# A two-layer spectral and MLP kernel: four plain groups instead of six, statistics scratch in PSUM, and a new order of the second pair's products

## The chip, the cores and the metric

One Trainium2 chip, one of its NeuronCores. The metric is the device time of one execution in microseconds (us). Engines are called PE (TensorE), DVE (VectorE), ACT (ScalarE), POOL (GpSimd) and SP (the queue that issues most DMAs).

## What is computed

The input x has 2048 tokens of 1024 features, in bf16. Four blocks follow one another, each added to its input: a spectral filter A, an MLP B, A again, and B again with the same weights.

```python
def _A_ref(x, w_r, w_i):
    X = rfft2(x, axes=(-2, -1))          # over tokens and features
    return irfft2(X * (w_r + 1j * w_i), s=(S, D)).astype(bf16)

def _B_ref(x, w1, b1, w2):               # D = 1024, F = 3584
    h = einsum("bsd,df->bsf", x, w1) + b1
    act = h * tanh(log1p(exp(-abs(h))) + where(h > 0, h, 0))   # Mish
    return einsum("bsf,fd->bsd", act, w2)

x = x + _A_ref(_layernorm(x), w_r, w_i)
x = x + _B_ref(_layernorm(x), w1, b1, w2)
x = x + _A_ref(_layernorm(x), w_r, w_i)
x = x + _B_ref(_layernorm(x), w1, b1, w2)
```

## The kernel before, in words

**Order and waits.** The program is written out by hand in one order; every engine gets its instructions in that order and runs them one after the other. A small class (Res) records who wrote and who read each buffer, and each instruction gets the semaphore waits that follow. DMAs queue in the same way on the engine that issues them: one that waits holds back all behind it on that queue.

**Tiles.** x stays in on-chip memory as 16 tiles of 128 tokens (XS). Layer B works on chunks of four tiles (512 tokens): pair 1 is chunks 0 and 1 (tiles 0 to 7), pair 2 chunks 2 and 3. A tile is normalised by statistics (stats_dve on DVE or stats_act on ACT, sums_to_mv, scales or root) and apply, and is then transposed into XT, by PE (transposed, L1109) or by DMA (normal, turned and turn).

**Hidden stage.** F is cut into 14 groups of 256. In pair 1, groups 0 to 5 are plain: mm1 (L1148) multiplies one chunk, 16 matmuls of 512 columns or twice as many of 256, and ACT applies Mish (L1152). These use banks 0 to 2 in rotation. Groups 6 to 13 of pair 1, and all 14 of pair 2, use Strassen's scheme in Winograd's form (quads): seven products of four 512-column matmuls (L1186), on sums of weight blocks (S1 to S4) and of token blocks (T1 to T4), in place of eight. A11, A12, A21 and A22 are the weight blocks, B11 and B21 the two halves of the first chunk, B22 a half of the second. DVE combines the products (add, L1191), ACT copies the first product out of its bank (L574) and applies Mish (L1196). token_sums (L1163) forms T1 to T4 on DVE from both chunks; T3 overwrites a part of the second chunk, so it waits until the plain products have read it.

**Weight sums.** In the first layer POOL makes S1 to S4 for each group with four additions (L1081 in fill_slot) and stores the slot to w1s_scratch; the second layer only loads it. For pair 1 the first four slots (early) lie where the tile of the inverse transform (UT) was, the next three (ws) where the plain weights were. POOL's first addition waits for a "gate", the normalisation of tiles 6 and 7 on DVE.

**Output stage.** products multiplies the hidden values by w2, again with seven Strassen products as stages of 4 tiles x 14 matmuls (L1268). STD and BACK are orders of these stages, BACK for pair 2 of the first layer. A stage's last product completes a half of a tile: in BACK B21 (stage 6) completes chunk 2 and T4 (stage 7) chunk 3. extra then takes statistics, normalises the tile, writes it to xn_scratch from POOL (xn_store) and reads it back from SP in the order that the next transform wants (xr_load, into XR); the last tile is copied there directly by 16 small DMAs (xr_direct). Meanwhile spin keeps PE busy with filler matmuls (L652). The next layer's first transform (s1, L635) reads XR in two halves and is drained by ACT (L641) and DVE (L643).

Of the kernel before, what the change touches and what calls it, by code (L numbers as in the profile page):

```python
# [7 lines left out]
P = 128  # L8
# [172 lines left out]
class KB:  # L181
# [274 lines left out]
    def sums_to_mv(self, j0, n):  # L456

        rs = self.r_mv[j0:j0 + n]
        mv, sq = self.MV[:, j0:j0 + n, :], self.RS[:, 1, j0:j0 + n]
        rr = self.r_rs[j0:j0 + n]  # L460

        def on(fn):
            self.op(self.dve, fn, reads=rs, writes=rs + rr)
        on(lambda e: e.tensor_scalar(mv, self.BN[:, j0:j0 + n, 0:2], 1.0 / self.D, None, op0=ALU.mult))
        on(lambda e: e.tensor_tensor(sq, mv[:, :, 0], mv[:, :, 0], ALU.mult))
        on(lambda e: e.tensor_tensor(mv[:, :, 1], mv[:, :, 1], sq, ALU.subtract))
# [27 lines left out]
    def scales(self, j0, n):  # L494

        rr = self.r_rs[j0:j0 + n]
        h, a, r = (self.RS[:, i, j0:j0 + n] for i in range(3))
        var = self.MV[:, j0:j0 + n, 1]
# [42 lines left out]
    def xr_load(self, j):  # L541
        self.dma(self.sp, self.XR.ap[row_of(j, 0):row_of(j, 7) + 1:4, :, :], self.xn_d[j], f"xl{j % 4}",
                 reads=[self.r_xnd[j]], parts=self.r_xr[1:3])

    def xr_direct(self, j, b, parts, queues):

        i = 0
# [147 lines left out]
    def layer_A(self, li):  # L695
# [189 lines left out]
        def open_ut():  # L885
            self.UT = self.alloc("UT", o["UT"], [P, P])

            self.r_ut = self.sub_res(self.UT, "ut", 4, o["UT"], P * P * 2)
# [61 lines left out]
        self.w1_buf = [self.alloc(f"W1_{i}", (self.ob["WS"] + i * 4096, 140 * K)[i > 4], [8, 256]) for i in range(6)]  # L950
        for fg in range(6):
# [119 lines left out]
    def fill_slot(self, b, fg, after=()):  # L1071
# [5 lines left out]
        self.load_w1(b.raw, fg, [b.res])  # L1077
        A = lambda n: self.wblock(b, n)
# [6 lines left out]
    def layer_B(self, li, last):  # L1085
# [91 lines left out]

        def quads(fgs, slot_of, B, after, lead=None):

            sums = open_sums()  # L1180

            def product(n, bank, a, b, start):
# [5 lines left out]
                            for db in range(4)], reads=[s.res, s.rs] + list(res), writes=[self.r_bank[bank]])  # L1188
# [9 lines left out]

            def parts(n):
                a, b, d = (3 * (n % 2) + i for i in range(3))  # L1200
                return a, b, d, sums[n % 2], sums[2 + n % 2], sums[4], 2 * fgs[n]

            N = len(fgs)
            for n in range(N + 1):
                if n < N:
                    a, b, d, p1, u2, u3, ft = parts(n)
                    product(n, a, "A11", "B11", True)
                    self.copy(act, p1.ap, PS[:, a, :], [self.r_bank[a]], [p1.res])
                    product(n, b, "S2", "T2", True)
                    add(u2, b, p1)  # L1210
                if n == N and lead:
                    lead()
                if n:
                    _, pb, pd, q1, q2, q3, pft = parts(n - 1)
                    mish(1, pft + 1, q3.ap, q3.res)
                    product(n - 1, pb, "A22", "T4", False)
                    add(q1, pb, q1)
                    mish(0, pft + 1, q1.ap, q1.res)
                    product(n - 1, pd, "S4", "B22", False)
                    add(q2, pd, q2)  # L1220
                    mish(1, pft, q2.ap, q2.res)
                    after(n - 1)
                if n < N:
                    product(n, d, "S1", "T1", True)
                    product(n, a, "A12", "B21", False)
                    mish(0, ft, PS[:, a, :], self.r_bank[a])
                    product(n, b, "S3", "T3", False)
                    add(u3, b, p1)
                    add(u3, d, u3)
# [7 lines left out]
        def load_w2(name, k, slot, prog=sp):  # L1237
# [5 lines left out]
            else:  # L1243
# [7 lines left out]
        BACK = (("A11", "B11", 0, True), ("S", "T3", 1, True), ("A21", "T1", 0, True), ("A11", "T2", 1, True), ("S", "B22", 0, False),  # L1251
                ("A12", "B21", 0, True), ("A22", "T4", 1, False))
# [181 lines left out]
        for j in range(4, 8):  # L1434
            residual(j)
# [5 lines left out]
        for fg in range(1, 4):  # L1441
            mm1(0, fg, 1)
            if fg > 1:
                self.stats_act(4 + fg)
        mm1(0, 4)
        at_tiles(1)
        mm1(0, 5, mid=turns(1, 0, 1))
# [6 lines left out]
        early = self.open_slots("WE", self.ob["W2"], 0, 1, 2, 3)  # L1454
        for n in range(4):
            self.fill_slot(early[n], 6 + n, [gate])
        for fg in range(2):
            mm1(1, fg, 0, mid=turns(1, 2, 3) if fg else ())
        for fg in range(2):
# [7 lines left out]
        for fg in range(2, 6):  # L1467
            if fg in (2, 4, 5):
                ws += self.open_slots("WS", self.ob["WS"], len(ws))
                self.fill_slot(ws[-1], 9 + len(ws))  # L1470
            mm1(1, fg)
            if fg == 2:
                token_sums(0, last=False)
            if fg == 3:
                for j in range(8, 12):
                    residual(j)
        order = early + ws + early[:1]
        B = token_sums(0)
        self.xn_buf = self.xn_out + [self.alloc(f"XN{i}", self.ob["XN2"] + i * 2048, [self.D]) for i in range(2)]

        def after(n):
            if n == 0:
                self.fill_slot(order[7], 13)
            if 1 <= n < 4:
                load_b(STD, n // 3, (n - 1) % 2)
            if n < 4:
                self.stats_dve(8 + n)
            if n == 4:
                self.scales(8, 4)
            if n > 3:  # L1490
                normal(4 + n)
                turn(4)
            for j in ((), (), (), (), (), (12, 13), (14,), (15,))[n]:
                residual(j)
        quads(list(range(6, 14)), order, B, after, lead)
        self.junk = self.alloc("JUNK2", self.ob["JUNK2"], [self.D])
        self.xn_buf = [self.alloc(f"XN{i}", self.ob["XN12"] + i * 2048, [self.D]) for i in range(2)] + self.xn_out
        w2 = {}
# [150 lines left out]
```

## Time and profile before

| quantity | value |
|---|---|
| median of 3 runs | 938.51 us (937.23 to 938.64) |
| the profiled execution | 936.66 us |
| its span, first to last instruction | 934.9 us |
| granted PE clock | 0.987 of full |
| first layer B, from the first plain product to the last output product | 122 to 476 us |
| pair 1's Strassen hidden stage, first layer | 172 to 223 us |
| from the last product to the second layer A's first transform | 476 to 488 us |
| second layer B, from the first plain product | 579 to 933 us |

The timeline gives start and duration of runs of like instructions; "x24" is their number, and the bracket says how long the engine had been idle before and what ended that. In the chain of work, each piece is what released the next one. "mean ns" of a matmul is longer than its step, because matmuls are pipelined; the step comes from a run of them divided by their number. SPq is the DMA-issuing part of SP.

### The profile page before, as it was taken

Reading aid. Unit: us, or ns where it says so; the run is one execution under the profiler, and the core shown is the slowest. Engines: PE = TensorE matmul, PEld = TensorE weight load, DVE = VectorE, ACT = ScalarE, POOL = GpSimd, SP = SyncE. Lnnn points to the kernel's source line nnn. Section 1 sums busy time; section 2 is a strip of 40 time slices with the busy share of each in tenths; the row PEclk is TensorE's granted clock in tenths of the full one; section 3 lists DMA queues with packets and bytes.
Section 4 is the critical chain, followed back from the end, with each engine's and each line's share of the span. In section 5 each row is a group of like instructions: output and inputs, shape, how many; then the busy total and the mean of one; then the engine's idle time right before and its main releaser. Section 6 shows DMA issues by size and latency. Waiting matters only on the chain.

```text
span 934.9 us, 13481 instructions
## 1 busy us (share of the span) xinstructions
PE 875.9 (94%) x5473; PEld 471.7 (50%) x5473; DVE 619.1 (66%) x973; ACT 427.5 (46%) x623; POOL 159.0 (17%) x183
## 2 busy tenths in 40 slices
PE   0799799999999999999979987999999999999998
PEld 0577486444444444444437765754444444444443
DVE  7698468686889667568746865647746665554473
ACT  7798485456203485510008975745551015552000
POOL 4922004950005642000130200000000000000000
PEclk9999999999999999999999997999999999999999
DMA  9969854676895488274640797433255635832432
GB/s 288 265 227 300 204 151 131 216 249 171 268 274 196 164 314 296 91 261 142 241 133 32 227 228 196 158 118 119 54 190 175 207 113 193 279 118 78 171 127 110
DMA packets 146335, 174.68 MB, mean 187 GB/s; under 512 B 66248, under 2 KB 125736, under 8 KB 146152
## 3 DMA queue, kind: packets, MB, share of 16 engines
q1 hardware_dynamic: 133424, 127.48, 44.5%
q0 software_dynamic: 10672, 44.67, 13.4%
q10 hardware_dynamic: 2176, 1.66, 0.6%
q8 instruction: 43, 0.70, 0.3%
q14 instruction: 20, 0.16, 0.0%
HBM read 130.00 MB, written 40.89 MB: 183 GB/s over the span
## 4 chain that ended last, share of the span: by engine, by line
PE 83%; DMA 5%; DVE 5%; ACT 2%; SPq 2%; POOL 1%; issue 1%; DVEq 0%; ACTq 0%; POOLq 0%
PE PS L1268 35%; PE PS L1186 28%; PE PS L1148 9%; SPq L251 2%; PE PS L799 2%; PE PS L725 2%; PE PS L824 2%; PE PS L1020 2%; POOL ARENA L1081 1%; PE PS L1109 1%; DMA ARENA<-in_A_x_dram 1%; DMA ARENA<-c_bt 1%; DMA ARENA<-u_scratch 1%; DMA u_scratch<-ARENA 1%; PE PS L635 1%; ACT ARENA L641 1%
## 5 line engine op out<-in xcount | busy, mean ns | idle before, releaser
L1268 PE MATMUL PS<-ARENA 128*128 128x512 bf16 x1568 | 340.1, 379 | 0.0
L1186 PE MATMUL PS<-ARENA 128*128 128x512 f16 (+1 forms) x1232 | 267.8, 379 | 0.4 <-POOL ARENA L1081 0.3
L1268 PEld LDWEIGHTS PS<-ARENA 128*128 128x128 bf16 x1568 | 153.4, 98 | 184.5
L1191 DVE TENSOR_TENSOR ARENA<-PS,ARENA 128x512 f32<-128x512 f32 x220 | 151.7, 691 | 95.7 <-PE PS L1186 90.7
L1186 PEld LDWEIGHTS PS<-ARENA 128*128 128x128 bf16 x1232 | 120.1, 98 | 146.8 <-POOL ARENA L1081 2.2
L1196 ACT ACTIVATE ARENA<-ARENA,B 128x512 bf16<-128x512 f32 x132 | 95.1, 721 | 66.5 <-DVE ARENA L1191 60.6
L574 ACT ACTIVATE ARENA<-PS 128x512 f32<-128x512 f32 (+2 forms) x82 | 61.1, 745 | 119.1 <-PE PS L1186 96.4
L1148 PE MATMUL PS<-ARENA 128*128 128x256 bf16 (+1 forms) x576 | 86.7, 308 | 0.3
L1081 POOL TENSOR_TENSOR ARENA<-ARENA 128x512 bf16<-128x512 bf16 x56 | 71.4, 1274 | 72.6 <-DVE ARENA L524 58.3
L453 ACT ACTIVATE ARENA<-XS 128x1024 bf16<-128x1024 bf16 x52 | 54.8, 1053 | 36.5 <-DVE XS L1319 33.0
L1148 PEld LDWEIGHTS PS<-ARENA 128*128 128x128 bf16 x576 | 55.2, 98 | 26.7 <-DVE ARENA L1114 1.0
L1293 DVE TENSOR_TENSOR ARENA<-ARENA 128x3584 bf16<-128x3584 bf16 x32 | 63.9, 2018 | 0.0
L1319 DVE TENSOR_TENSOR XS<-PS,ARENA 128x512 bf16<-128x512 f32 x52 | 35.7, 690 | 38.9 <-PE PS L1268 38.7
L1152 ACT ACTIVATE ARENA<-PS,B 128x256 bf16<-128x256 f32 (+1 forms) x72 | 38.3, 542 | 35.3 <-PE PS L1148 34.8
L1311 DVE TENSOR_TENSOR ARENA<-PS,ARENA 128x512 f32<-128x512 f32 x48 | 32.9, 688 | 28.9 <-PE PS L1268 28.4
L1196 ACT ACTIVATE ARENA<-PS,B 128x512 bf16<-128x512 f32 x44 | 30.2, 686 | 18.0 <-PE PS L1186 18.0
L1307 DVE TENSOR_TENSOR ARENA<-ARENA,XS 128x512 f32<-128x512 f32 x52 | 36.7, 731 | 0.5
L1163 DVE TENSOR_TENSOR ARENA<-ARENA 128x2048 f16<-128x2048 bf16 x16 | 25.3, 1582 | 17.6 <-PE PS L1148 17.3
L799 PE MATMUL PS<-ARENA 128*128 128x256 bf16 x256 | 32.4, 273 | 3.9 <-DVE ARENA L788 3.2
L472 DVE BATCH_NORM_STATS2 BN<-XS 128x6 f32<-128x512 bf16 x52 | 32.6, 669 | 4.5 <-DMA XS<-in_A_x_dram 4.5
L444 ACT ACTIVATE RS<-MV,EPS 128x1 f32<-128x1 f32 (+2 forms) x11 | 3.3, 296 | 70.7 <-DVE MV L565 70.0
L777 ACT ACTIVATE ARENA<-PS 128x1024 bf16<-128x1024 f32 x32 | 33.3, 1071 | 4.5 <-PE PS L773 4.5
(97 smaller groups left out, 820.9 us busy)
## 6 DMA issues: line engine op xcount, KB each, us to landing
ARENA<-in_B_w_dram SPq DMA_DIRECT2D x30, 896.0 KB, 6.4
ARENA<-w1s_scratch SPq DMA_DIRECT2D x30, 896.0 KB, 4.7
ARENA<-w2s_scratch SPq DMA_DIRECT2D x24, 896.0 KB, 6.7
ARENA<-in_B_w_dram SPq DMA_DIRECT2D x26, 512.0 KB, 5.2
w1s_scratch<-ARENA POOLq DMA_DIRECT2D x14, 896.0 KB, 4.2
u_scratch<-ARENA SPq DMA_DIRECT2D x14, 512.0 KB, 3.5
ARENA<-u_scratch SPq DMA_DIRECT2D x14, 512.0 KB, 5.9
w2s_scratch<-ARENA POOLq DMA_DIRECT2D x8, 896.0 KB, 4.1
```

The costliest lines, as they stand in the source:

```text
L453: self.op(act, lambda e, i=i, f=f: e.activation(junk.ap, x, f, accum_out=sums[:, i:i + 1]), reads=[self.r_xs[j]], writes=[junk.res], parts ...
L574: fn = (lambda e: e.activation(dst, src, ACT.Copy)) if scale is None else \
L799: fns.append(lambda e, c=c, part=part: e.matmul(ps[:, c * 256:(c + 1) * 256], yk.ap[:, part, c * P:(c + 1) * P], t[:, (128, 0)[part]:(384, ...
L1081: self.op(self.pool, lambda e, dst=A(dst), x=A(x), y=A(y), op=op: e.tensor_tensor(dst, x, y, op), reads=[b.res] + list(after), writes=[b.rs])
L1148: fns.append(lambda e, db=db, bank=bank, fl=fl: e.matmul(PS[:, bank, 0:w], wb.ap[:, db, fl * P:(fl + 1) * P], x.ap[:, db, tok], start=(db ...
L1152: self.op(act, lambda e, bank=bank, ft=ft, at=at: e.activation(at[:, tok], PS[:, bank, 0:w], ACT.Mish, bias=self.B1[:, ft:ft + 1]), reads= ...
L1186: self.group([lambda e, db=db: e.matmul(PS[:, bank, :], A[:, db, :], mov[:, db, :], start=(start and db == 0), stop=(db == 3), skip_group_ ...
L1191: self.op(dve, lambda e: e.tensor_tensor(dst.ap, PS[:, bank, :], x.ap, ALU.add), reads=[self.r_bank[bank], x.res], writes=[dst.res])
L1196: self.op(act, lambda e: e.activation(at, src, ACT.Mish, bias=self.B1[:, ft:ft + 1]), reads=[res, self.r_b1], writes=[ra])
L1268: self.group([lambda e, i=i, k=k, b=PB[n][k].ap: e.matmul(PS[:, bank, :], ap[:, i, t * P:(t + 1) * P], b[:, i - 7 * k, :], start=(start an ...
L1293: self.op(dve, lambda e: e.tensor_tensor(ap[dst][:, f, :], ap[x][:, f, :], ap[y][:, f, :], op), reads=part(x, k) + part(y, k), writes=part ...
L1307: self.op(dve, lambda e: e.tensor_tensor(a[t], a[t], x, ALU.add), reads=[rx], writes=[r[t]])
```

## The change

1. Pair 1 has four plain groups (0 to 3) and ten Strassen groups (4 to 13). quads is split into block (the product A11 x B11 and its copy), corner (A12 x B21 and its Mish) and run (the rest). Blocks of the first four Strassen groups, and corners of three, need chunk 0 alone and are issued before chunk 1 is transposed; the fourth corner is issued in run. Four banks and two further buffers hold them.
2. The raw weights of these four groups are loaded earlier (fill_raw), the sums made or loaded later (fill_sums). UT is tracked in quarters.
3. Statistics of tiles 8 to 11 go from DVE to ACT; their scales, and the squares in sums_to_mv, use PSUM bank 7 as scratch. Residual additions are spread otherwise, tiles 6 and 7 come before 4 and 5.
4. In the second layer, tiles 13 and 14 are transposed by DMA instead of PE.
5. BACK is reordered: T4 becomes the fifth stage, B21 the last. Chunk 3 is completed in the fifth stage, chunk 2 in the last. The last but one tile is copied directly too, the tile before it is read back from POOL's queue, and the queues of the direct copies are chosen anew. spin has 38 matmuls instead of 24.

```diff
-    def scales(self, j0, n):
+    def scales(self, j0, n, bank=None):
...
+        if bank is not None:
+            a, rr = self.PS[:, bank, 0:n], rr + [self.r_bank[bank]]
...
-            self.r_ut = self.sub_res(self.UT, "ut", 4, o["UT"], P * P * 2)
+            self.r_ut = [self.sub_res(self.UT, f"ut{q}", 1, o["UT"] + P * 64 * q, P * 64)[0] for q in range(4)]
...
+    def fill_raw(self, b, fg):
+
+        r = self.r_w1d[fg]
+        if r.writes:
+            self.dma(self.sp, b.ap[:, 0:2048], self.w1s_d[fg][:, 0:2048], f"w1_{b.res.name}", reads=[r], writes=[b.res])
+        else:
+            self.load_w1(b.raw, fg, [b.res])
+
+    def fill_sums(self, b, fg, after):
+
+        r = self.r_w1d[fg]
+        if r.writes:
+            self.dma(self.sp, b.ap[:, 2048:3584], self.w1s_d[fg][:, 2048:3584], f"w1s_{b.res.name}", reads=[r], writes=[b.rs])
+        else:
+            self.w1_sums(b, fg, after)
...
+            def block(n, bank=None):
+                a, b, d, p1, u2, u3, ft = parts(n)
+                a = a if bank is None else bank
+                product(n, a, "A11", "B11", True)
+                self.copy(act, p1.ap, PS[:, a, :], [self.r_bank[a]], [p1.res])
+
+            def corner(n, bank=None):
+                a, b, d, p1, u2, u3, ft = parts(n)
+                a = a if bank is None else bank
+                product(n, a, "A12", "B21", False)
+                mish(0, ft, PS[:, a, :], self.r_bank[a])
...
-        BACK = (("A11", "B11", 0, True), ("S", "T3", 1, True), ("A21", "T1", 0, True), ("A11", "T2", 1, True), ("S", "B22", 0, False),
-                ("A12", "B21", 0, True), ("A22", "T4", 1, False))
+        BACK = (("A11", "B11", 0, True), ("S", "T3", 1, True), ("A21", "T1", 0, True), ("A11", "T2", 1, True), ("A22", "T4", 1, False),
+                ("S", "B22", 0, False), ("A12", "B21", 1, True))
...
         for fg in range(1, 4):
             mm1(0, fg, 1)
-            if fg > 1:
-                self.stats_act(4 + fg)
-        mm1(0, 4)
+            if fg < 3:
+                self.stats_act(5 + fg)
         at_tiles(1)
-        mm1(0, 5, mid=turns(1, 0, 1))
...
+        for n, bank in ((0, 3), (1, 4), (2, 5), (3, 0)):
+            block(n, bank)
+        corner(1, 4)
+        turns(1, 0)[0]()
+        corner(2, 5)
+        turns(1, 1)[0]()
+        corner(3, 0)
         self.sums_to_mv(6, 2)
         self.scales(6, 2)
...
-        for fg in range(2):
-            mm1(1, fg, 0, mid=turns(1, 2, 3) if fg else ())
-        for fg in range(2):
+            self.fill_sums(early[n], 4 + n, [gate])
+        for fg in range(3):
+            mm1(1, fg, 0, mid=turns(1, 2, 3) if fg == 2 else ())
+        for fg in range(3):
             mm1(1, fg, 1)
...
-            if n < 4:
-                self.stats_dve(8 + n)
-            if n == 4:
-                self.scales(8, 4)
-            if n > 3:
-                normal(4 + n)
+            if n in (0, 2, 4, 5):
+                self.stats_act(8 + (0, 2, 4, 5).index(n))
...
+            if n in (5, 7):
+                self.sums_to_mv(n + 3, 2, 7)
+                self.scales(n + 3, 2, 7)
+            if n > 5:
+                normal(2 + n)
                 turn(4)
...
+        by_pe = 15 if last else 13
...
-            if n >= 5:
-                j = 4 * n - 12 + t
+            if n == 5 and t == 0:
+                self.xr_load(15)
+            if n in (4, 6):
+                j = 4 * (n == 4) + 8 + t
                 self.stats_second(j, 0, False)
                 self.root(j, 1)
                 b = self.apply(j, out=True)
-                if j < 15:
+                if j == 10:
+                    self.xr_direct(j, b, 1, (pool, sp))
+                    self.xr_load(9, pool)
+                elif j == 11:
+                    self.xr_direct(j, b, 2, (act, pool, sp, act, pool, act, pool, sp) * 2)
+                else:
                     self.xn_store(j, b)
-                if j > 8:
-                    self.xr_load(j - 1)
-                if j == 15:
-                    self.xr_direct(j, b, 2, (pool, act, sp))
+                    if t:
+                        self.xr_load(j - 1)
         products(1, self.ob["XT2"], stages, extra)
         if not last:
-            self.spin(24, 7)
+            self.spin(38, 7)
```

## The prediction

> **What bounds the kernel now.** I read the page's busy shares first, then the chain of work that ended last in order of time, then the timelines round the three places that the diff touches. First the page:
>
> ```profile
> PE 875.9 (94%) x5473; PEld 471.7 (50%) x5473; DVE 619.1 (66%) x973; ACT 427.5 (46%) x623; POOL 159.0 (17%) x183
> ```
>
> TensorE (PE) is the bound: 94% busy. So two things shorten the run: fewer PE instructions, or less of the 59 us in which PE is idle. The chain, in order of time, shows that the Strassen hidden stage is solid PE, and it shows the largest hole, between the second pair's last product and the next layer's first transform:
>
> ```profile
> 172.05 46.62 PE PS L1186 x216
> ...
> 476.99 3.62 DMA xn_scratch<-ARENA
> 480.63 0.60 SPq L251
> 481.85 6.10 DMA ARENA<-ARENA
> 488.19 5.29 PE PS L635 x48
> 493.51 6.53 ACT ARENA L641 x7
> 500.18 1.05 PE PS L725 x8
> ```
>
> 46.62/216 gives **0.2158 us** for a 512-column matmul. Then: tile 14's store lands at 480.61, SP can only then issue its reload and, behind it, its share of tile 15's direct copies; one of them lands at 487.95; L635 runs 48 matmuls of 128 columns in 5.29 us (0.110 each); after that the ACT evictions of L641 are the chain up to 500.18. The PE timeline of the same place:
>
> ```profile
> 469.68 6.85 PE L1268 MATMUL PS<-ARENA 128*128 128x512 bf16 x31
> 476.37 5.34 PE L652 MATMUL PS<-BD 128*128 128x512 bf16 x24
> 488.19 8.85 PE L635 MATMUL PS<-M,ARENA 128*128 128x128 bf16 x104 [6.48 <-DMA ARENA<-ARENA]
> ```
>
> The 24 filler matmuls of spin (L652) take 5.34 us (0.2225 each); then PE is idle for 6.48 us.
>
> Third, POOL where the first pair's Strassen stage begins (a sum op, L1081, x4 is one slot):
>
> ```profile
> 152.45 6.57 POOL L1081 TENSOR_TENSOR ARENA<-ARENA 128x512 bf16<-128x512 bf16 x4 [58.35 <-DVE ARENA L524]
> 159.32 0.56 POOL L251 DMA_DIRECT2D w1s_scratch<-ARENA  x1 [0.30 <-POOL ARENA L1081]
> 159.89 5.90 POOL L1081 TENSOR_TENSOR ARENA<-ARENA 128x512 bf16<-128x512 bf16 x4
> 166.09 0.57 POOL L251 DMA_DIRECT2D w1s_scratch<-ARENA  x1 [0.30 <-POOL ARENA L1081]
> 166.68 4.85 POOL L1081 TENSOR_TENSOR ARENA<-ARENA 128x512 bf16<-128x512 bf16 x4
> ```
>
> A slot costs 4.85 us undisturbed and up to 6.57 while DVE is adding; with store and gap a turn is 5.7 to 6.9 us. POOL has its first slot ready 13 us before PE needs it at 172.05. This lead is what the change spends.
>
> [...] after 6.48 us idle, 0.110 us per matmul for 5.29 us, while later tiles keep pace with the evictions. [...] 6.57 against 4.85 us for a slot. [...] SP needs 3.20 us for five direct copies.
>
> **The change part by part**, against the profiled execution: 936.66 us with a span of 934.9; it lies 1.85 below the median of 938.51.
>
> *(a) Two plain groups become Strassen groups.* A plain group of the first pair is 32 matmuls of 512 columns (or their half-width equal), a Strassen group 28. Two groups, so 8 x 0.2158 = **-1.73 us a layer**, on the path. Eight products (four blocks, the corners of 1 to 3 and of 0) change place; seven run before chunk 1 is there.
>
> *(b) The one-chunk stretch.* From 142.10 to 172.05 PE now takes 29.95 us for 29.73 us of work (0.2 of waits). Afterwards ACT has moved: statistics of tile 6 come one group earlier, so L1152's activations of group 2 wait behind them (from 139.43, 2.23 us), and with three rotating banks the second half of group 3 waits until 142.1: 0.9 us. The four new bank copies (L574, 0.60 each) come after tile 7's statistics, so the first corner waits for the second copy: 0.25. Reuse of bank 0 and the last transposes' copies 0.2 to 0.3. Sum 1.4, less the 0.2 of today: +1.2. Net with (a): **-0.5 a layer**, the quads then starting at about 165.6 instead of 172.05 with 252 matmuls (54.4 us) left instead of 224 (48.3 us). What hides what is left of ACT's extra work is 7 us of PE. If no wait appears, it is -1.9; if each is twice as long, +0.9.
>
> *(c) Less cover behind it, layer 0.* The gate for POOL falls at about 153.7 (scales of tiles 6 and 7 end later). The last token sum (L1163, 2.50 us at 172.16, POOL active) starts when plain group 3 ends, at 165.6, ends at 168.2; the add of group 0 sits behind it on DVE (0.69), and S3xT3 needs both: PE would be there at 168.15 and starts at 169.0, **+0.85**. Then POOL: slot ready times 159.9, 166.7, 172.8, 178.6, 184.3, 190.0 (turns of 6.8 while token sums and residuals run, 5.7 after). PE needs the sums of groups 1 to 5 at 169.9, 174.2, 178.5, 183.7 and 190.4 (groups 1 to 3 are only 20 matmuls, 4.32 us): late by 0.1 and 0.6, **+0.8** with the sequencer's gap. The tenth slot is ready at 213.0, needed at 213.9. Ends: 0 and +3.5. Layer 1 loads the sums by DMA, and there L1163 takes 1.23 us: nothing.
>
> *(d) Loads.* Two plain weight buffers go; four raw loads come from SP before the residuals. Tracking the u tile in quarters lets the first go out at 127.9 (quarters 0 and 1 read) instead of 137.1; the last two still start at 137.1 and, at the listed 5.2 us to landing, arrive by 143, when PE reaches block 2 at 144.8. Hidden by the plain groups; without it about 1 us. In layer 1 the split loads are 8 instead of 4 issues on SP, hidden by the same.
>
> *(e) Statistics of tiles 8 to 11 to ACT, residuals spread, scratch in a bank.* ACT in a full group: 3.4 us plus 2.23 of 6.04; in the 20-matmul groups 2.2 + 2.23 against 4.32, 0.1 late, and banks are double-buffered: nothing. PSUM scratch has no row here[...]. Between 0 and +0.3 on the path; I take 0.
>
> *(f) Tiles 13 and 14 of layer 1 turned by DMA.* 16 transposes of 1.34/24 us leave PE: **-0.9**. SP gets 16 transposes of 1.26 us (20 us), in front of weight loads and output stores. Those loads are for two stages (24 us) ahead, and SP has gaps by 720: hidden; bounds -0.9 and +0.5.
>
> *(g) BACK order and the transition.* Chunk 3 is finished at stage 5 (A22xT4), so its four stores and reloads leave the end, and only chunk 2 is there. DVE's cycle of 2.77 in 3.02 us is the same, and A22xT4 reuses banks drained 9 us earlier: no wait. On SP the reloads of 12 to 14 wait for their stores (3.6 us) in stage 4, with stage 6's weight load behind the first two; that is needed 12 us later, so nothing. At the end, with today's clock: last apply ends 479.35 as now. Tile 10's direct copies go on POOL (477.0 to 479.1) and SP (to 479.0), tile 9's reload goes on POOL at 479.1 without waiting (its store landed at 477.5), and tile 11's copies on ACT (from 479.4, 0.70 each), POOL (from 479.65, 0.54) and SP (from 479.4, 0.64), no longer behind a store. The eight that complete the first half are issued by 481.5; with 3.1 us (ACT) and 3.8 (POOL) to landing the half is there at about 484.6. Spin of 38 x 0.2225 = 8.45 ends at 484.8. So s1 starts at 484.9 instead of 488.2 (**-3.3**), and warm: the evictions, not 0.110 us matmuls, set its pace; 1.1 us to the first ACT eviction plus 9 x 0.95 ends at 494.6, before 500.0. I count 1.7 of these 2.2 us, as the second half lands only near 487. Sum **-5.0**; ends -6 and -1 (the spin alone would cost +3.1 were the data ready at once, but it never is).
>
> Sum: -0.5 - 0.5 + 1.65 - 0.9 - 5.0 = **-5.25**: 931.4 profiled, 933.3 as median.
>
> **Rivals.** *Slower: POOL's pace in layer 0.* Ten slots instead of eight, with 6 us less lead. If every turn takes 7.0 us (today's disturbed ones took 6.6 to 6.9), the tenth is ready at 222.8 against a need of 213.9: +8.9 in place of +0.8, sum +2.85, **941.4**. It decides from turns of about 6.7 on average. For it: residuals, applies and the T3 sum now fall among POOL's turns. Against it: adds from PSUM left slots at 4.86 us. *The transition gives nothing:* tile 9's reload, also a whole 256 KB, delays the direct copies as tile 14's does now; only 0.3 remains: -0.55, **938.0**. *No new waits:* ACT and DVE keep up: -3.45 - 0.9 - 5.0 = -9.4, **929.1**. That the change isn't what it says: the 3.5 us of matmuls would stay; the code excludes it.
>
> **How the numbers follow.** Forecast 0.65, no new waits 0.15, no transition gain 0.13, POOL's pace 0.07. About 0.2% (1.9 us) is what a measurement of this kernel can tell from no change; so faster 0.80, same 0.13, slower 0.07. The range of 929 to 938 runs from the case without waits to that without a transition gain, and leaves out POOL's case and the outer ends.
>
> **What would show it.** PE time of L1186 and L1148 together down by 16 x 0.2158 = 3.5 us, 16 transposes fewer. Right: s1 starts 8.5 us after the last product, its matmuls at the eviction pace from the first; L1186 waits for POOL under 1.5 us. Wrong: PE idle over 2 us between spin and s1, slots over 6.7 us apart, PE waits on ACT over 2 us between 140 and 150, or SP late with stage loads in layer 1.

## The result, and the profile after

The changed kernel takes 936.6 us (median of four runs, 936.35 to 939.16) against 938.07 us for the kernel before in the same comparison: a ratio of 0.9991 with a 95% interval of 0.9972 to 1.0011. A repeat below, with more runs, gives 0.9996 [0.9985, 1.0006]. So a gain of 5.2 us was forecast, and about 1 us or nothing came.

The profiled execution (939.16 us, span 937.4) is the slowest of the four. Single spans can't be compared: with the same code up to there, the mark at which the table below begins lies at 139.06 us in one run and at 142.48 in another. Stretches between two marks on PE are compared instead.

The page's first row:

```profile
PE 876.4 (93%) x5487; PEld 471.6 (50%) x5487; DVE 623.5 (67%) x997; ACT 444.0 (47%) x661; POOL 159.6 (17%) x187
```

PE's busy sum has not fallen, although the groups changed as intended: the line of the quads' products has 1344 matmuls for 1232 (+112, which is 2 groups x 2 layers x 28), the plain line 480 for 576, more of them of half width. The sum can't show the 3.5 us saved: the 14 additional filler matmuls (3.1 us) are busy time too, and ends of matmuls are modelled (a matmul of the quads lasts 379 ns on the page, and a row of 88 of them below takes 19.15 us, 218 ns each). So the time is looked for in stretches.

The stretch of the four plain groups and the quads in the first layer, on PE's timeline:

```profile
143.55 1.05 PE L1172 MATMUL PS<-ARENA 128*128 128x256 bf16 x8 [0.62 <-ACT ARENA L1176]
...
185.34 19.15 PE L1212 MATMUL PS<-ARENA 128*128 128x512 f16 x88 [0.74 <-POOL ARENA L1105]
205.92 16.58 PE L1212 MATMUL PS<-ARENA 128*128 128x512 f16 x76 [1.43 <-DVE ARENA L1217]
```

The first two waits are those of the forecast's steps (b) and (c). The third, 1.43 us behind a DVE add of quads, was not in it. POOL's slots are not the cause; on its timeline the turns about that time are 6.07 and 5.75 us (its stores between them are left out here):

```profile
179.99 5.20 POOL L1105 TENSOR_TENSOR ARENA<-ARENA 128x512 bf16<-128x512 bf16 x4
186.06 4.87 POOL L1105 TENSOR_TENSOR ARENA<-ARENA 128x512 bf16<-128x512 bf16 x4
191.81 5.20 POOL L1105 TENSOR_TENSOR ARENA<-ARENA 128x512 bf16<-128x512 bf16 x4
```

The end of the first layer's output stage and the transition, on PE's timeline:

```profile
469.56 1.67 PE L1311 MATMUL PS<-ARENA 128*128 128x512 bf16 x7 [1.37 <-DMA ARENA<-in_B_w_dram]
471.86 10.75 PE L1311 MATMUL PS<-ARENA 128*128 128x512 bf16 x49 [0.62 <-DMA ARENA<-in_B_w_dram]
482.44 8.36 PE L655 MATMUL PS<-BD 128*128 128x512 bf16 x38
492.31 6.83 PE L638 MATMUL PS<-M,ARENA 128*128 128x128 bf16 x104 [1.50 <-DMA ARENA<-ARENA]
```

The idle time ahead of the transform has gone from 6.48 to 1.50 us, 3.0 of it filled with filler, and its 104 matmuls run in 6.83 us in place of 8.85: the granted clock is 1.00 over the transform, where it was 0.50 for the transform's first 5.2 us in the kernel before. But the stage before it now waits twice for its weights, 2.0 us. The chain of work through the same place:

```profile
462.52 9.29 DMA ARENA<-in_B_w_dram
...
479.98 5.22 DMA xn_scratch<-ARENA
...
485.49 0.55 POOL ARENA L251
...
486.16 1.08 POOL ARENA L251 x2
487.25 4.61 DMA ARENA<-ARENA
...
496.47 5.61 ACT ARENA L644 x6
```

Weights issued at 462 take 9.3 us to land; tile 9's store takes 5.2 us, POOL issues tile 9's reload at 485.49, when that store has landed, and direct copies behind it from 486.16, and one of them lands at 491.9. Evictions on ACT end the chain, as before.

Between marks, in us against the kernel before (before; the changed kernel; its repeat; forecast):

| stretch | before | changed | repeat | forecast |
|---|---|---|---|---|
| layer 1: chunk 0's last plain products to pair 1's first output product | 81.59 | +2.34 | +2.34 | +1.15 |
| to pair 2's first output product | 171.53 | -0.08 | -0.98 | 0 |
| to its last product | 86.33 | +2.33 | +2.11 | 0 |
| to the first transform | 11.82 | -1.95 | -1.70 | -3.3 |
| the first transform | 11.99 | -2.08 | -2.08 | -1.7 |
| layer 2: as the first row | 81.59 | -0.42 | -0.42 | -0.5 |
| to pair 2's first output product | 170.56 | +0.55 | -0.03 | -0.9 |
| sum | | +0.69 | -0.76 | -5.25 |

The repeat's -0.76 agrees with its median, 937.45 against 938.1. The fourth row leans on one profile of the kernel before. Two runs below with the same end (pair1_alone and narrow_wait) have 11.03 and 11.10 us there, so the 11.82 is a long one, and the earlier start is worth 0.9 to 1.95 us.

### The profile page after: what moved, and what is told of

The parts are those of the page before. It is cut to its first block, busy times and chain, and to the rows that moved or that the text cites. A ratio compares the mean times of both kernels' runs of the same rounds, so it can differ in the third digit from the quotient of the medians.

```text
span 937.4 us, 13600 instructions
## 1 busy us (share of the span) xinstructions
PE 876.4 (93%) x5487; PEld 471.6 (50%) x5487; DVE 623.5 (67%) x997; ACT 444.0 (47%) x661; POOL 159.6 (17%) x187
## 4 chain that ended last, share of the span: by engine, by line
PE 75%; DMA 8%; DVE 7%; POOL 4%; ACT 4%; issue 1%; SPq 1%; DVEq 0%; POOLq 0%; ACTq 0%
PE PS L1311 34%; PE PS L1212 27%; PE PS L1172 3%; POOL ARENA L1105 3%; PE PS L802 2%; PE PS L728 2%; PE PS L1023 2%; PE PS L827 2%; DMA XS<-in_A_x_dram 1%; POOL ARENA L251 1%; PE PS L1133 1%; DMA ARENA<-c_bt 1%; DMA ARENA<-in_B_w_dram 1%; DMA ARENA<-w1s_scratch 1%; DMA ARENA<-w2s_scratch 1%
## 5 line engine op out<-in xcount | busy, mean ns | idle before, releaser
L1212 PE MATMUL PS<-ARENA 128*128 128x512 f16 (+1 forms) x1344 | 293.8, 379 | 3.0 <-DVE ARENA L1217 1.4
L1217 DVE TENSOR_TENSOR ARENA<-PS,ARENA 128x512 f32<-128x512 f32 x240 | 163.0, 690 | 103.9 <-PE PS L1212 95.1
L1222 ACT ACTIVATE ARENA<-ARENA,B 128x512 bf16<-128x512 f32 x144 | 103.0, 720 | 72.2 <-DVE ARENA L1217 67.0
L453 ACT ACTIVATE ARENA<-XS 128x1024 bf16<-128x1024 bf16 x68 | 71.6, 1052 | 37.3 <-DVE XS L1362 33.0
L1336 DVE TENSOR_TENSOR ARENA<-ARENA 128x3584 bf16<-128x3584 bf16 x32 | 63.9, 2017 | 0.0
L1172 PE MATMUL PS<-ARENA 128*128 128x256 bf16 (+1 forms) x480 | 59.9, 281 | 1.4 <-ACT ARENA L1176 1.2
L1354 DVE TENSOR_TENSOR ARENA<-PS,ARENA 128x512 f32<-128x512 f32 x48 | 32.9, 688 | 28.2 <-PE PS L1311 27.8
L1222 ACT ACTIVATE ARENA<-PS,B 128x512 bf16<-128x512 f32 x48 | 32.9, 684 | 19.0 <-PE PS L1212 19.0
L1176 ACT ACTIVATE ARENA<-PS,B 128x256 bf16<-128x256 f32 (+1 forms) x60 | 28.4, 484 | 20.6 <-PE PS L1172 20.4
L784 DVE TENSOR_TENSOR ARENA<-ARENA 128x1024 bf16<-128x1024 bf16 x32 | 22.0, 687 | 21.3 <-ACT ARENA L780 15.6
L728 PE MATMUL PS<-FD,ARENA 128*128 128x256 bf16 (+1 forms) x256 | 31.8, 271 | 2.5 <-ACT ARENA L644 1.3
```

Of the source, the lines that this page charges most:

```text
L453: self.op(act, lambda e, i=i, f=f: e.activation(junk.ap, x, f, accum_out=sums[:, i:i + 1]), reads=[self.r_xs[j]], writes=[junk.res], parts ...
L728: fns.append(lambda e: e.matmul(dst, at(r), FD[:, t:t + n], start=start, stop=stop))
L1172: fns.append(lambda e, db=db, bank=bank, fl=fl: e.matmul(PS[:, bank, 0:w], wb.ap[:, db, fl * P:(fl + 1) * P], x.ap[:, db, tok], start=(db ...
L1212: self.group([lambda e, db=db: e.matmul(PS[:, bank, :], A[:, db, :], mov[:, db, :], start=(start and db == 0), stop=(db == 3), skip_group_ ...
L1217: self.op(dve, lambda e: e.tensor_tensor(dst.ap, PS[:, bank, :], x.ap, ALU.add), reads=[self.r_bank[bank], x.res], writes=[dst.res])
L1222: self.op(act, lambda e: e.activation(at, src, ACT.Mish, bias=self.B1[:, ft:ft + 1]), reads=[res, self.r_b1], writes=[ra])
```

## The experiments

All ratios are to the kernel before, with 95% intervals. The first three runs split the change.

**The changed kernel again** (no edit).

> The changed kernel once more, to tell what repeats from what was this one profile. Theory (waits that the order of the program makes): the same waits come back within 0.3 us: PE about 0.7 us for a weight-sum slot of POOL and 1.4 us for DVE near 205 in the first layer, 2.0 us for the weight load of the second pair's last stage, 1.5 us at the first transform, 1.1 us for the same stage's load in the second layer; time 936 to 937, 0.997 to 0.999 of before. Rival (a bad draw): the DMA waits of this profile, 3.1 us together, are chance and shrink to under 1 us, and the profiled time falls to about 936.

937.45 us, 0.9996 [0.9985, 1.0006], the table's third column of times. The waits are there again, 1.41 us for DVE, 1.31 and 0.46 for the last stage's weights in layer 1 and 0.69 for them in layer 2, so they belong to the kernel; the 0.9 us in the second row (a wait for w1s) is not.

**The second pair's end alone**, on the kernel before:

```diff
+        BACK = (... ("A22", "T4", 1, False), ("S", "B22", 0, False), ("A12", "B21", 1, True))
+            if n == 5 and t == 0:
+                self.xr_load(15)
+            if n in (4, 6):
+                j = 4 * (n == 4) + 8 + t
...
-            self.spin(24, 7)
+            self.spin(38, 7)
```

> The kernel before with the new BACK order alone (stage order, reloads, direct copies, 38 filler matmuls). Theory: 4.0 us gained from the last product to the end of the first transform, 2.0 lost waiting for the last stage's weights: 2 us faster than before, about 936. Rival (the whole change's gain is here and undisturbed): no wait for weights when pair 1 is as before, 4 to 5 us faster, about 933.5.

936.94 us, 0.9989 [0.9982, 0.9996]: 1.2 us below the kernel before, where 2 was expected. Its last stage +1.80, start of the transform -2.02, transform -2.08: the two gains are there, and most of one is paid back in the stage before.

**All but that** (the changed kernel with BACK, its extra and spin as before):

> The kernel before with all but the BACK part: four plain groups, one-chunk products, statistics on ACT, bank scratch, two tiles of the second layer by DMA transposes. Theory: first layer +2.3, second layer -0.4 in the hidden stage and +0.5 in the output stage, together 2.4 us slower, about 940.5. Rival (my forecast of these parts was right and the profile a bad draw): -0.3 in all, about 938.

938.54 us, 1.0004 [0.9994, 1.0013]. The two halves of the change are about +0.4 and -1.2 us in median. In the profile: +2.34, -0.97, -0.42, and -0.90 for the tiles turned by DMA, so here step (f) is whole. That is why it isn't 2.4 us slower, as expected: the second row (see narrow_wait below) and step (f) bring 0.9 us each. Start-up scatter is larger than what is left.

**Two waits mended, and four.** two_mends issues each reload of chunk 3 a stage later, and gives every small DVE operation of tiles 8 to 11's scales a PSUM operand. four_mends also leaves tiles 13 and 14 to PE and copies tile 9 directly:

```diff
-            if n == 5 and t == 0:
-                self.xr_load(15)
+            if n == 5:
+                self.xr_load(12 + t)
...
-                    if t:
+                    if t and n == 6:
                         self.xr_load(j - 1)
...
+            on(lambda e: e.tensor_scalar(hp, var, 0.5, 0.5e-5, op0=ALU.mult, op1=ALU.add))
+            on(lambda e: e.tensor_copy(r, rp))
+            for i in range(2):
+                on(lambda e: e.tensor_tensor(a, rp, r, ALU.mult))
+                on(lambda e: e.tensor_tensor(a, hp, a, ALU.mult))
...
-        by_pe = 15 if last else 13
+        by_pe = 13
...
+                if j == 9:
+                    self.xr_direct(j, b, 1, (pool, sp, pool, act))
+                    self.xr_load(8)
```

(The lines after the third "..." are in four_mends alone.)

> The changed kernel with two of the four mends only: chunk 3's reloads behind the last stage's weight load on SP, and the scales with their operands in the bank. Theory: the order of SP's queue made that wait [...], so 2.1 and 0.9 go and the transition keeps its 9.9 and 9.9 us (to the first transform and through it): 3.0 us below the changed kernel, about 934.4. Rival (the reloads, now later, collide with the end of the stage as they may have in the run with four mends): the transition goes back to 11.8 and 12.2 us and the kernel is no faster than 937.

> The changed kernel with four mends, one for each wait: chunk 3's reloads follow the last stage's weight load on SP; tiles 13 and 14 of the second layer back to PE; the scales of tiles 8 to 11 with at most one operand on chip memory's side (the rest in the bank); tile 9 copied directly, so that POOL waits for no store. Theory: 2.0 + 0.5 + 1.3 + 1.5 us less, 5 us below the changed kernel, about 931.5. Rival (the waits only move to the next thing: DMA bandwidth, POOL's pace): under 2 us less, 935 or more.

two_mends: 934.35 us, 0.9964 [0.9953, 0.9975]. four_mends: 938.62 us, 1.0001 [0.9991, 1.001]. PE's timeline of two_mends:

```profile
184.36 31.24 PE L1235 MATMUL PS<-ARENA 128*128 128x512 f16 x141 [0.73 <-POOL ARENA L1128]
216.05 4.49 PE L1235 MATMUL PS<-ARENA 128*128 128x512 f16 x20 [0.45 <-DVE ARENA L1240]
...
439.71 37.72 PE L1334 MATMUL PS<-ARENA 128*128 128x512 bf16 x170
477.26 8.37 PE L678 MATMUL PS<-BD 128*128 128x512 bf16 x37
487.14 6.83 PE L661 MATMUL PS<-M,ARENA 128*128 128x128 bf16 x104 [1.51 <-DMA ARENA<-ARENA]
```

The wait of 1.43 near 205 is gone. Another of 0.45, which the changed kernel doesn't have, stands at 216 behind the second pair of scales; what makes it is not shown. The first row of the table becomes +1.36, 0.98 less, and the output stage runs without a break (+0.00, 2.1 us less). The two edits act in stretches of their own, so each has its own number. four_mends was a miss: with direct copies of tile 9 added, the transform waits longer for a copy: it starts 11.83 us after the last product, for 9.88 in two_mends. PE is idle for 3.46 us and the transform runs cold, that is at little more than half pace at first (its first 20 matmuls in 2.29 us, where two_mends has 76 in 5.03), in all 12.23 us in place of 9.91, so the transition gives nothing; its tiles 13 and 14 on PE take the 0.9 us of step (f) back.

```profile
490.02 9.10 PE L661 MATMUL PS<-M,ARENA 128*128 128x128 bf16 x104 [3.46 <-DMA ARENA<-ARENA]
```

**The transition's parts**, each on two_mends: tile 9 read back from SP's queue in place of POOL's; tiles 9 to 11 stored, reloaded and copied as the kernel before does, in the new order of stages; 24 fillers.

```diff
-                    self.xr_load(9, pool)
+                    self.xr_load(9)
```
```diff
-                if j == 10:
-                    self.xr_direct(j, b, 1, (pool, sp))
...
+                if t and n == 6:
+                    self.xr_load(j - 1)
+                if j == 11:
+                    self.xr_direct(j, b, 2, (pool, act, sp))
```
```diff
-            self.spin(38, 7)
+            self.spin(24, 7)
```

> Two mends, and tile 9's reload on SP's queue instead of POOL's. If the issue of the copies that complete the first half sets the start of the first transform (POOL's were held behind the reload), all are issued 1.1 us earlier and the start comes 0.8 to 1.1 us earlier, at 8.9 us after the last product. If their landing does[...], it moves by less than 0.3.

> Two mends, and the end as before the change: tiles 8 to 10 stored and reloaded from SP, tile 11 alone copied directly, queues in the old turn; 38 filler matmuls stay. If the direct copy of tile 10 and the new queues bring the earlier start, it goes back to about 11.8 us after the last product (idle 3.4 us behind the filler, so the transform also runs cold, 12 us). If the earlier finish of chunk 3 brings it, it stays near 9.9.

> Two mends, with 24 filler matmuls as before the change. If the filler keeps the array's clock up and so makes the transform short, the start stays at 9.9 us after the last product, PE is idle for 4.5 us before it and the transform takes 12 us instead of 9.9: 2.1 us slower than with 38. If the transform is short because its input comes in another order, it stays at 9.9.

reload9_sp: 933.04 us, 0.9947 [0.9929, 0.9965]; the transform starts 9.61 us after the last product, for 9.88 in two_mends. That isn't shown to be more than scatter: seven profiles with the reload on POOL's queue have 9.80 to 10.12, four with it on SP's 9.54 to 10.40. The edit also did less than intended: POOL's copies of tile 11 start 3.28 us after the last product for 3.67, not 1.1 sooner, and SP's now stand behind the reload.

old_end: 936.11 us, 0.998 [0.9973, 0.9987]; the start is 11.21 us, so direct copies and queues bring 1.3 us of it, and the idle 2.84 us costs 1.26 in the transform. Three profiles with the old order of stages too have 11.03 to 11.82, so finishing chunk 3 earlier shows no gain of its own.

two_spin24: 935.79 us, 0.9971 [0.9961, 0.998]; the start stays at 9.95, and the transform takes 11.92 us. PE's timeline of two_spin24:

```profile
478.74 5.34 PE L678 MATMUL PS<-BD 128*128 128x512 bf16 x24
488.69 8.79 PE L661 MATMUL PS<-M,ARENA 128*128 128x128 bf16 x104 [4.60 <-DMA ARENA<-ARENA]
```

With nothing else changed, the 14 further filler matmuls keep the transform at its pace: up to 492 us it has 76 matmuls in 5.03 us with them (0.066 each) and 32 in 3.57 without (0.112). This is worth 2.0 us of this stretch.

**One line of the kernel before**: in product, only products on S1 to S4 wait for the weight sums.

```diff
-                            for db in range(4)], reads=[s.res, s.rs] + list(res), writes=[self.r_bank[bank]])
+                            for db in range(4)], reads=[s.res] + [s.rs] * (a[0] == "S") + list(res), writes=[self.r_bank[bank]])
```

> The kernel before with one line of the change: a product waits for the weight sums only if its weight block is one (S1 to S4). Theory: this is where 0.98 us of the second pair of the first layer went, since there PE stood at the second group's first product, which needs no sum: 0.9 to 1.0 us less between the two pairs' output stages (171.5 to 170.6), nothing elsewhere. Rival (POOL has fewer slots to fill in the second pair, four for six): no change from this line.

937.65 us, 0.9988 [0.9978, 0.9999]; the second row of the table is -0.98, as in every kernel that has the line but the profiled changed one, which lost it to a wait for w1s. PE's timeline of before, and then of narrow_wait:

```profile
311.00 34.30 PE L1186 MATMUL PS<-ARENA 128*128 128x512 bf16 x156 [0.34 <-POOL ARENA L1081]
```
```profile
309.00 36.21 PE L1186 MATMUL PS<-ARENA 128*128 128x512 bf16 x164
```

The product A11 x B11 of a group waited for POOL's sums though it reads none. The change contains this line, and the forecast didn't see it.

**The scratch of the scales back in on-chip memory** (changed kernel, reloads mended):

```diff
-                self.sums_to_mv(n + 3, 2, 7)
-                self.scales(n + 3, 2, 7)
+                self.sums_to_mv(n + 3, 2)
+                self.scales(n + 3, 2)
```

> The changed kernel with the reloads behind the last stage's weight load, and the scales' scratch back in on-chip memory (no bank). If DVE operations with two operands there are held while POOL adds, more of the eleven wait, and the first layer's hidden stage of pair 1 takes longer than with the scratch in the bank (83.9 us): 84.5 to 86. If the scratch does not matter, 83.9. The second layer, where POOL is idle, gains up to 0.3 from the shorter operations.

939.11 us, 1.0006 [0.9997, 1.0014]; the first row is +7.22 us (88.8 us, above the 84.5 to 86 expected), 4.9 more than with the bank. In the second layer, where POOL doesn't add, the row is -0.42 with the bank and without it: the expected gain of up to 0.3 didn't come, and the loss goes with POOL's additions. DVE's timeline of no_bank, while POOL adds and after it has ended (216 us):

```profile
204.50 1.61 DVE L515 TENSOR_TENSOR RS<-RS 128x2 f32<-128x2 f32 x1
206.34 1.00 DVE L517 SCALAR_TENSOR_TENSOR RS<-RS 128x2 f32<-128x2 f32 x1
...
221.62 0.16 DVE L515 TENSOR_TENSOR RS<-RS 128x2 f32<-128x2 f32 x1
222.01 0.16 DVE L517 SCALAR_TENSOR_TENSOR RS<-RS 128x2 f32<-128x2 f32 x1
```

And DVE's timeline of the changed kernel, whose scratch is only partly in the bank:

```profile
201.98 0.82 DVE L504 TENSOR_SCALAR RS<-MV 128x2 f32<-128x2 f32 x1
203.03 0.17 DVE L515 TENSOR_TENSOR PS<-RS 128x2 f32<-128x2 f32 x1
203.63 1.22 DVE L515 TENSOR_TENSOR PS<-RS 128x2 f32<-128x2 f32 x1
```

The same operation on two values takes 0.16 us, or 1.0 to 1.2 where it meets one of POOL's additions (4.87/4 = 1.22 us each); the one of 1.61 started while POOL issued a store and ended with the addition behind it. Of the eleven operations for tiles 8 and 9 in no_bank, five took 0.74 us or more; the others started between two additions. L515 multiplies r by r: its output is in the bank, its inputs are not, and it is held all the same. In two_mends no such operation of these scales takes over 0.17. How much it costs varies: the profiled execution of no_bank is 2.2 us above that kernel's median, and in the medians no_bank is 0.42% (3.9 us) slower than two_mends, where the stretches of the table add up to 6.6.

**ACT's order ahead of the corners**, on reload9_sp: tile 6's statistics after group 2, tile 7's after the four block copies; act_order_bank0 also uses the bank in the first layer only.

```diff
-            if fg < 3:
-                self.stats_act(5 + fg)
+            if fg == 2:
+                self.stats_act(6)
...
+        self.stats_act(7)
```
```diff
-                self.sums_to_mv(n + 3, 2, 7)
-                self.scales(n + 3, 2, 7)
+                self.sums_to_mv(n + 3, 2, None if last else 7)
+                self.scales(n + 3, 2, None if last else 7)
```

> Two mends, tile 9's reload on SP, and ACT's order in the one-chunk stretch changed: statistics of tile 6 behind plain group 2 as before the change, those of tile 7 behind the four blocks' copies. If ACT's order made PE wait there (0.6 at the second half of plain group 3, 0.6 at the first corner and the block in bank 0), both layers' stretch from the first plain products to the output stage is 1.0 us shorter (83.0 to 82.0, 81.5 to 80.5). If what follows then waits for tile 7's statistics, or POOL for its later gate, the first layer gains nothing.

> The last one, with the bank scratch used in the first layer alone, where POOL adds at the same time. Theory: another 0.3 us less in the second layer (80.5 to 80.2); in all about 931, 7 us below the kernel before. Rival (the 0.3 us came from elsewhere): as the last one.

act_order: 932.96 us, 0.9946 [0.9931, 0.996]; act_order_bank0: 933.15 us, 0.9942 [0.9923, 0.9961]. On PE the order takes 0.7 (layer 1, 82.25 for 82.97) and 0.8 us (layer 2, 80.69 for 81.48), and the bank left out 0.3 more in layer 2 (80.38), where POOL does not add. act_order_bank0 was expected at about 931. Its profile loses 2.1 us at the transition against act_order's (10.40 and 11.15 us for 9.54 and 9.91) with the same code there: PE was idle for 2.03 us behind the filler. The medians don't tell these apart from reload9_sp.

**Output stores of pair 1, layer 2, on ACT's queue**: on the changed kernel, and on act_order_bank0.

```diff
-                    self.dma(sp, self.out[0, j * P:(j + 1) * P, 512 * h:512 * h + 512], x, "st", reads=[done])
+                    self.dma(sp if p else act, self.out[0, j * P:(j + 1) * P, 512 * h:512 * h + 512], x, "st", reads=[done])
```

> The changed kernel with one edit: the first pair's output stores of the second layer are issued on ACT's queue and no longer on SP's. If SP's queue is what holds stage 7's load of the second layer (the transposes of a step take some 2.4 us of it and the stores 0.58, against about 3.0 us of products a step), the load is issued right when its buffer comes free, some 4 us earlier than at 745 us in the changed kernel, PE doesn't wait for it, and the stretch from the first to the second output stage of layer 2 is 169.7 us in place of 171.1 and 170.5: about 0.9 to 1.4 us less in all than the changed kernel, some 935.5 to 936.5. The rival, that the load lands late because the DMA engines are loaded: the load is issued early, takes more than its 8 to 9 us, and the wait stays: 936.6 to 937.5.

> act_order_bank0 with the same edit of the output stores. That kernel showed no wait for stage 7's load (169.66 us), so where SP's queue is the cause the edit brings nothing here but safety: 932.5 to 933.2. If the stores on ACT's queue hold up ACT (its evictions of the second pair), the stretch from the first to the second output stage of layer 2 grows above 169.7 us, and the time to 934 or more.

stores_alone: 936.49 us, 0.9984 [0.9974, 0.9993]; all_in: 931.64 us, 0.9918 [0.9904, 0.9932]. The table's last row becomes 169.65 (-0.91) in stores_alone. SP's timeline of the changed kernel (transposes and stores alternate, then stage 7's load), and PE's:

```profile
742.09 2.37 SPq L250 DMA_TRANSPOSE ARENA<-FD  x2
744.50 0.58 SPq L251 DMA_DIRECT2D out_dram<-XS  x1
745.12 1.74 SPq L251 DMA_DIRECT2D ARENA<-w2s_scratch  x2
```
```profile
752.16 1.68 PE L1311 MATMUL PS<-ARENA 128*128 128x512 bf16 x7 [0.48 <-DMA ARENA<-w2s_scratch]
754.47 10.75 PE L1311 MATMUL PS<-ARENA 128*128 128x512 bf16 x49 [0.63 <-DMA ARENA<-w2s_scratch]
```

SP's timeline of stores_alone, and PE's:

```profile
739.16 1.11 SPq L251 DMA_DIRECT2D ARENA<-w2s_scratch  x2
```
```profile
744.75 17.43 PE L1311 MATMUL PS<-ARENA 128*128 128x512 bf16 x80
```

Counted from the first output product of the layer, the load goes out 4.4 us earlier (63.9 for 68.3), and PE waits for nothing. So SP's queue is what made the load late. A slow landing (8.83 us) has its share in the wait: in seven other kernels with the same queue the load goes out 66.8 to 67.6 us after the first output product and PE waits for nothing. In all_in the edit costs nothing that shows (169.66 in the last row); its interval overlaps that of act_order_bank0, so it isn't shown to be faster than that. It has the lowest median of all runs, 6.7 us below the kernel before, and its stretches add up to -6.4.

## Why the prediction was wrong, step by step

The forecast missed by 4.5 us on the repeat's sum: +2.11 (output order), +1.19 (first layer), +0.87 (loads in layer 2), +1.6 - 0.38 (transition), +0.08, and -0.98 that it hadn't seen. The steps that failed are the cost of the scratch in (e), "hidden" in (f), "nothing" for the queue in (g), the start of the transform in (g), and T3's wait in (c), which didn't come; the rest below held or nearly so. The measured time lies within the stated range, near the end that was to stand for a transition without gain, but other losses brought it there.

*(a), (b)* held: -0.42 for -0.5 in layer 2, where nothing else is in the stretch. The wait for ACT after group 2 is the one described, and act_order shows that 0.7 to 0.8 of (b)'s 1.2 us was avoidable.

*(c)* held for POOL and not for T3. PE waits 0.74 for POOL where 0.8 was forecast. POOL's first two turns took 6.58 and 7.31 us (the kernel before has one of 7.44, which the prediction's "5.7 to 6.9" leaves out), the others 5.7 to 6.1, the mean 6.1, so the slower rival (turns of 6.7 on average) has no support. The +0.85 for T3 didn't come: the last token sum (L1187 on DVE, at 166.80) took 1.86 us where 2.50 was taken, and PE's row of 80 matmuls from 166.53 has no break, 18.07 us for 17.26 of work, so what it lost there is in small pieces.

*(d)* held: PE does not wait for raw loads.

*(e)* failed. "Between 0 and +0.3 on the path; I take 0" was the author's estimate of what the scratch itself costs, with no row of the kernel before behind it. What costs time is POOL: operations that read two operands from on-chip memory (up to 1.22 us in the changed kernel), and those of L464 and L504 (0.73 and 0.82), are held to the end of an addition when they meet one, where they take 0.16 to 0.17 alone. The prediction had seen that POOL's slots grow from 4.85 to 6.57 us while DVE is adding, and it used this for POOL's slots alone, not for DVE's small operations. Between the profiles of no_bank and two_mends this is 5.9 us in this stretch, of which the change takes 4.9 and leaves 0.98. The remainder of the first layer is +1.36 against +1.15, and that this is close is in part luck: T3's 0.85 is missing from it, and the wait of 0.45 at 216 was not forecast.

*(f)* had the mechanism right, and its bound of -0.9 is what comes wherever the load is in time. It failed in "hidden": per step SP issues two transposes in 2.37 us and a store in 0.58, 2.95 of the 3.02 us that a step takes, so the "gaps" which it saw were used up and the load lay behind: it goes out 66.8 to 68.3 us after the first output product, for 64.8 in the kernel before. With 7 to 8 us left the wait is 0.7 to 1.1 us in three kernels (8.8 us to landing in two of them; in the repeat the load's second half went out later still), none in seven others.

*(g), queue order,* failed. "With stage 6's weight load behind the first two; that is needed 12 us later, so nothing." The order is as it says, eight old reloads and two new ones ahead of the load (SP's timeline of the changed kernel), but the second new one waits for tile 13's store:

```profile
444.48 17.50 SPq L251 DMA_DIRECT2D ARENA<-xn_scratch  x10
462.02 1.06 SPq L251 DMA_DIRECT2D ARENA<-in_B_w_dram  x2
463.12 17.13 SPq L251 DMA_DIRECT2D ARENA<-xn_scratch  x3
```

In two_mends the load goes out 60.8 us after pair 2's first output product (at 451.77), here 68.2, and it lands 9.3 us later. Such stores took 6.7 us to land in this stretch (median) where 3.6 was taken. This is the 2.1 us that two_mends takes away.

*(g), transition:* the warm part was right in kind and a little small (-2.08 for -1.7); two_spin24 shows that it is the filler. The start was at 9.87 us after the last product, not 8.5, so -1.7 to -1.95 (or less, see the table) for -3.3. Two terms failed. One is "without waiting (its store landed at 477.5)": the store took 5.22 us to land where 3.6 was taken, POOL waited 0.48 for it, and its first copy of tile 11 went out 3.72 us after the last product, for 3.28. The larger one is the landing: POOL's copy that ends the wait took 4.61 us where 3.8 was forecast. These are 0.4 and 0.8 of the 1.4 us. Moving the reload to SP showed no gain, and four_mends, with tile 9's copies added, made it worse. What sets a copy's landing here is not settled: size, queue and DMA load weren't varied singly.

The rival with no transition gain named the right place, a reload ahead of the copies, yet 3.8 of 5.0 us came. Of its other rivals none is supported.

## What to carry to other kernels

When a DMA is moved, list every queue it is issued on with the waits of each entry, and ask which load stands behind it: two of the losses here (2.1 us, and up to 1.1) were weight loads that stood behind other entries of SP's queue. Where GpSimd adds, count DVE's tiny operations by the operation they may be held for, not by their own length (here up to 1.61 us for 0.16). Filler ahead of a stage was worth what the array's pace was worth over the next stage (2.0 us here), and only where it ended close to the data: the transform kept its pace after holes of up to 1.75 us (6.83 us for 104 matmuls) and lost it after 2.03 (8.01).

## What had not been expected of the hardware

- A DVE operation on 128x2 values took 0.16 us alone, and 0.82 to 1.61 us where POOL's additions held it; with an input in PSUM 0.16 to 0.17 in every such row of the changed kernel's and two_mends' first layer. An output in PSUM alone didn't help where both inputs lay in on-chip memory (1.22). The scratch itself cost at most 0.3 us in the second layer (act_order 80.69 us with it, act_order_bank0 80.38 without, no difference in no_bank).
- The time of the transform's first 104 matmuls by the idle time ahead of them: 6.83 us after 1.17 to 1.75, 8.01 after 2.03 (act_order_bank0), 8.04 after 2.84 (old_end), 9.10 after 3.46, 8.79 after 4.60, 8.85 after 6.48. The granted clock is 0.50 from 489.7 to 493.1 in old_end, about 3.4 us, and from 486.6 to 493.4 in the kernel before, about 6.8 us, of which the transform's first 5.2 us fall into it, and 1.00 on either side. Up to 492 us, the transform has 42 matmuls in 3.71 us (0.088 each) in act_order_bank0, 24 in 2.62 (0.109) in old_end, 20 in 2.29 (0.115) in four_mends, 32 in 3.57 (0.112) in two_spin24 and 37 in 4.11 (0.111) in the kernel before, where two_mends has 76 in 5.03 (0.066). So a hole of 2.03 us was enough to slow the transform, and after 6.48 us the low clock lasted longer than after 2.84 (6.8 us for 3.4). Why a hole of 2.03 us is enough isn't shown.
